# Reordering the last loads and the output projection at the end of a cached-attention decode step

## The chip, the cores and the metric

The kernel runs on one core of one Trainium2 chip. The metric is the device time of one execution in microseconds (us). The profile takes one execution; its own span is about 1.2 to 1.4 us shorter than the time of the same run. All times of events below are us from the start of that span.

Words used throughout: the attention works on half-tiles of K and V of 4 MB (4 heads of one batch row, a half of their positions). **P0** and **P1** are the last two of 32 half-tiles. In each half-tile some of the 128 key columns (positions per partition) get their scores on TensorE (transpose, copy by ScalarE, matmul with q) and the rest on VectorE (multiply, four halving adds, one reduce). A **group** is 8 key columns on TensorE. **P·V** is the matmul of the exponentials with V, the **projection** the matmul of the earlier heads' output with wo, and **gate**, **up** and **down** are the three FFN products. The earlier heads' output is the tile O_all. The **granted clock** is TensorE's clock as a share of its full speed: 1.00 is called full clock here, 0.50 half clock.

## The reference

```
h  = x + attention(layernorm(x)) @ wo      # 2 batch rows, 1 query each, 32 heads x 128,
                                           # 8192 cached keys and values per head, bf16
h2 = h + (relu(n @ W_gate) * (n @ W_up)) @ W_down    # n = layernorm(h), 512 -> 1376 -> 512
```

K and V are 268 MB of the 281 MB that have to be read, and every byte is used once.

## The kernel before

A loop works off 15 pairs of half-tiles; the last pair is written out behind it (the "tail"). The parts that matter, cut (`...`):

```python
# SP queue: loads of the last pair (o is the last pair; X is freed by VectorE of the loop)
load(K, A_k_cache, o, k_sem[0], 0, J)                   # first half of K: P0
sp.wait((d2s, 2 * o))
nc.sync.dma_start(X[:], A_wo[0:128 * DR]...)            # wo, 3.5 MB
load(K, A_k_cache, o, k_sem[1], J, 2 * J)               # second half of K: P1
sp.wait(tokp("pv", p))
load(V, A_v_cache, o, v_sem, 0, J)                      # V of P0
for k, (j0, j1) in enumerate(((V_LAST, J), (0, V_LAST))):   # V_LAST = 32
    load(V, A_v_cache, o, sem_vl[k], J + j0, J + j1)
...                                                     # then W_up, W_gate, W_down
```

```python
# TensorE, tail
k_part(tail, P0, range(2, 7), ((k2p, 1),))              # 5 groups (40 columns)
k_part(tail, P1, range(8, 13), ((k2p, 2),))
nc.tensor.wait_ge(a2p, 14); nc.tensor.wait_ge(sem_wo, 16)
for r in range(DR): ... matmul(Op[1][...], lhsT=O_all[:, r, :], rhs=X[...])   # projection, 28
pv(tail, P0, ...)
nc.tensor.wait_ge(a2p, 16)
for c in range(DC): ... matmul(Wp[...], lhsT=os_sb[strided], rhs=sel2)       # its sum, fp32
pv(tail, P1, ...)
```

```python
# ScalarE, tail: in this order
# P0: copies of 5 groups, exponentials of TensorE's columns
# P1: copies of 5 groups, exponentials of TensorE's columns, copy of O_all,
#     exponentials of P0's VectorE columns, copy of the projection, exponentials of P1's
```

The softmax here doesn't subtract the row's maximum and nothing guards it: scores larger than these inputs give would overflow.

## Time and profile before

| | before |
|---|---|
| time, median of 3 runs | 657.40 us (657.39 to 657.51) |
| span of the profile | 656.1 us |
| DMA rate, 40 to 560 us | 434 GB/s, DMA share 1.00 |
| P1's last score on TensorE | 631.7 |
| last exponential | 639.4 |
| last matmul of P·V ends | 644.4 |
| gate matmuls start | 650.36, on a DMA |

The first lines to read are the DMA rate and the DMA share: the loop is a stream of bytes that never pauses. What the engines do can only matter behind the last bytes of K, and there the reader compares two clocks: when the weights land, and when the engines are ready for them. How the time from 639 to 656 is spent shows in the view by stretches (columns: stretch, its length, busy time of PE, PEld, DVE, ACT and POOL with instruction counts, granted TensorE clock, DMA share, GB/s):

```profile
639.00:644.00 5.00, 4.51 (x50) 2.98 (x46) 0.35 (x2) 0.42 (x4) 0.00 (x0) 1.00 0.98 408
650.00:656.00 6.00, 3.60 (x93) 2.53 (x90) 1.25 (x6) 0.54 (x2) 0.00 (x0) 0.50 0.39 144
```

While P·V runs, TensorE is busy 4.51 of 5 us at the full clock, and the DMA queue is still full; it drains only in the last 6 us. So at the end of this kernel the bytes and the engines are almost level.

### The profile page before, as it was taken

To read this page: it belongs to the slowest core of one execution; us is meant where nothing else is said; L and a number is where in the kernel's file an instruction comes from. 1 tells how busy PE (TensorE), PEld (TensorE's weight loads), DVE (VectorE), ACT (ScalarE), POOL (GpSimd) and SP (SyncE) were. 2 spreads that over 40 slices of the span, in tenths; PEclk is the share of its full clock that TensorE was granted. 3 is DMA by queue.
4 is the path that set the end of the run, shared out by engine and by line. 5 is a ranking of instruction groups with operands and counts; after the bars stand their busy time and mean duration, and the time that the engine had idled before them with its cause. 6 is when DMAs were issued, how large, how long until landed. Compare 5 with 4: busy or idle time off the path is not lost.

```text
span 656.1 us, 8543 instructions
## 1 busy us (share of the span) xinstructions
PE 371.9 (57%) x3480; PEld 236.3 (36%) x3481; DVE 432.7 (66%) x275; ACT 304.6 (46%) x719; POOL 88.7 (14%) x96
## 2 busy tenths in 40 slices
PE   2374573756457385545637555474755537464677
PEld 0152441615134161423416242251623325152445
DVE  1187493947849395793939669393875939488771
ACT  1355362735536173443716445371653527254460
POOL 4000020030301103030120303003030300303000
PEclk9856556566655756665575667557565655766657
DMA  9999999999999999999999999999999999999997
GB/s 408 401 439 440 447 435 404 443 443 443 416 428 439 447 439 400 443 443 447 420 420 439 447 435 404 447 439 447 428 412 443 443 435 420 431 439 415 430 423 313
DMA packets 6324, 281.16 MB, mean 429 GB/s; under 512 B 710, under 2 KB 812, under 8 KB 1324
## 3 DMA queue, kind: packets, MB, share of 16 engines
q1 hardware_dynamic: 6308, 281.05, 99.3%
q8 instruction: 5, 0.08, 0.1%
q14 instruction: 3, 0.02, 0.0%
q10 hardware_dynamic: 8, 0.00, 0.0%
HBM read 281.05 MB, written 0.00 MB: 428 GB/s over the span
## 4 chain that ended last, share of the span: by engine, by line
DMA 64%; PE 22%; ACT 7%; DVE 6%; issue 1%; DVEq 0%; SPq 0%
DMA K<-in_A_k_cache_dram 59%; PE T L395 16%; ACT kT L578 7%; DMA K<-in_B_W_gate_dram 5%; PE S L378 5%; DVE prod L552 2%; DVE prod L561 2%; DVE X L561 1%; DVE X L552 1%; DVE scores L566 0%; PE O L816 0%; PE O L764 0%; DVEq L617 0%; DVEq L598 0%; DVE kT L824 0%
## 5 line engine op out<-in xcount | busy, mean ns | idle before, releaser
L578 ACT ACTIVATE kT<-T 128x1024 bf16<-128x1024 bf16 x160 | 160.0, 1022 | 196.5 <-PE T L395 192.7
L395 PE MATMUL T<-ident_f,K 128*128 128x128 f32 x640 | 161.7, 416 | 100.7 <-DVEq L598 94.8
L552 DVE TENSOR_TENSOR X<-K,q_c 128x11264 bf16<-128x11264 bf16 x15 | 90.4, 6026 | 172.5 <-DMA K<-in_A_k_cache_dram 172.5
L418 PE MATMUL O<-V,e 128*16 128x512 bf16 x1024 | 117.2, 596 | 111.1 <-ACT e L506 77.0
L395 PEld LDWEIGHTS T<-ident_f,K 128*128 128x128 f32 x640 | 114.5, 213 | 102.8 <-DVEq L598 96.8
L561 DVE TENSOR_TENSOR prod<-prod 128x5632 bf16<-128x5632 bf16 (+1 forms) x68 | 104.3, 1533 | 4.0
L552 DVE TENSOR_TENSOR prod<-K,q_c 128x11264 bf16<-128x11264 bf16 x17 | 102.3, 6020 | 6.2 <-DMA K<-in_A_k_cache_dram 4.5
L506 ACT ACTIVATE e<-scores 32x88 bf16<-32x88 f32 x128 | 51.1, 399 | 105.4 <-DVEq L609 103.9
L418 PEld LDWEIGHTS O<-V,e 128*16 128x16 bf16 x1024 | 30.3, 116 | 184.9 <-ACT e L506 101.8
L561 DVE TENSOR_TENSOR X<-X 128x5632 bf16<-128x5632 bf16 (+3 forms) x60 | 92.0, 1533 | 3.7
L378 PE MATMUL S<-q_c,kT 128*128 128x8 bf16 x1280 | 60.8, 171 | 40.1 <-ACT kT L578 40.0
L378 PEld LDWEIGHTS S<-q_c,kT 128*128 128x128 bf16 x1280 | 51.5, 107 | 75.6 <-ACT kT L578 73.7
L533 POOL MEMSET O_l<- 128x32 bf16 x13 | 1.7, 130 | 427.6 <-DVEq L615 427.6
L538 POOL COPY rsel<-rows 128x112 bf16<-128x112 bf16 x14 | 40.4, 2885 | 39.5 <-DVEq L615 38.7
L431 PE MATMUL Ob<-sel,os_sb 128*128 128x4 f32 x136 | 29.3, 339 | 11.0 <-ACT os_sb L581 11.0
L506 ACT ACTIVATE e<-S 32x40 bf16<-32x40 f32 x128 | 31.9, 249 | 2.4 <-PE S L378 0.9
L431 PEld LDWEIGHTS Ob<-sel,os_sb 128*128 128x128 f32 x136 | 27.8, 303 | 12.9 <-ACT os_sb L581 12.8
L506 ACT ACTIVATION_READ_ACCUMULATOR e<-scores 32x1 f32 x128 | 28.1, 219 | 0.0
L506 ACT ACTIVATION_READ_ACCUMULATOR e<-S 32x1 f32 x128 | 25.6, 200 | 1.5
L540 POOL TENSOR_TENSOR O_l<-O_cur,mask 128x32 bf16<-128x32 bf16 x14 | 23.1, 1652 | 0.0
L549 POOL COPY q_c<-q_all 128x144 bf16<-128x144 bf16 x16 | 15.2, 950 | 45.5 <-PE O L418 33.1
L578 ACT ACT_TABLE_LOAD x15 | 19.2, 1283 | 0.3
(106 smaller groups left out, 136.2 us busy)
## 6 DMA issues: line engine op xcount, KB each, us to landing
K<-in_A_k_cache_dram SPq DMA_DIRECT2D x2, 4096.0 KB, 21.8
V<-in_A_wq_dram SPq DMA_DIRECT2D x1, 4096.0 KB, 12.5
V<-in_A_v_cache_dram SPq DMA_DIRECT2D x1, 4096.0 KB, 24.9
X<-in_A_wo_dram SPq DMA_DIRECT2D x1, 3584.0 KB, 18.0
V<-in_A_v_cache_dram SPq DMA_DIRECT2D x1, 3072.0 KB, 32.1
K<-in_B_W_up_dram SPq DMA_DIRECT2D x1, 1376.0 KB, 30.1
K<-in_B_W_gate_dram SPq DMA_DIRECT2D x1, 1376.0 KB, 33.1
V<-in_A_v_cache_dram SPq DMA_DIRECT2D x1, 1024.0 KB, 33.9
```

What stands on the lines that cost most here:

```text
L378: i = nc.tensor.matmul(Sp[p % 2][:, A * jj:A * jj + 2 * A], lhsT=kv_[:, k, r, :], rhs=q_c[:, 2 * A * r:2 * A * r + 2 * A], start=(r == 0), ...
L395: i = nc.tensor.transpose(Tp[g % 2][:, k * 128:(k + 1) * 128], k_t[:, j:j + 2, :].rearrange("p j d -> p (j d)").bitcast(F32), ident_f[:])
L418: i = nc.tensor.matmul(Op[0][c:c + 16, :], lhsT=e_t[q][:, j // VJ, :], rhs=v_t[:, j:j + VJ, :].rearrange("p j d -> p (j d)"), start=(q == ...
L431: i = nc.tensor.matmul(Ob[:, 0:A], lhsT=os_sb[:, jj * Dh:(jj + 1) * Dh], rhs=sel[:, A * jj:A * jj + A], start=(jj == 0), stop=(jj == VJ - 1))
L506: i = nc.scalar.activation(out=e_t[q][h, j0 // VJ:j1 // VJ, :].rearrange("p g (j a) -> p g j a", a=A)[:, :, :, a], in_=src(h, a), func=ACT ...
L533: pool.run(e.memset(o_window(o - 1)[0], 0.0))
L538: e.tensor_copy(out=rsel[:, :, o % B, :], in_=bass.AP(x.tensor, x.offset, [list(x.ap[0]), [DR - OS, A], [1, DR]]))
L540: e.tensor_tensor(out=w, in0=O_cur[:].unsqueeze(2).broadcast_to([128, A, NM]), in1=mask[:, off // 4:off // 4 + OS // 4 * (A - 1) + 1:OS // ...
L549: nc.gpsimd.tensor_copy(out=q_c[:], in_=q_all[:, o]).then_inc(g2d, 1)
L552: return nc.vector.tensor_tensor(out=pr[:, 0:JC, :], in0=tile(K, p)[:, 0:JC, :], in1=q_c[:, Q2:QW].unsqueeze(1).broadcast_to([128, JC, Dh] ...
L561: run(nc.vector.tensor_tensor(out=pr[:, 0:JC, 0:w], in0=pr[:, 0:JC, 0:w], in1=pr[:, 0:JC, w:2 * w], op=ALU.add))
L578: to_pe(nc.scalar.activation(out=kT[gg % 2][:], in_=Tp[gg % 2][:].bitcast(BF16), func=ACT.Copy))
```

## The change

Its intent: keep the last K in one piece ahead of wo, so that the key work of both last half-tiles can run without a second wait for K; put the projection of the earlier heads between the two key parts; and take 16 of VectorE's columns of P1 over to TensorE (7 groups, 56 columns) so that VectorE ends earlier. The last V keeps its pieces of 32, 24 and 8 KB a row, with the small piece now at the other end of the columns. At the very end each engine that copies the output waits for its own slice of the last matmul group. The core of the diff (cut):

```diff
-                k_part(tail, P0, range(2, 7), ((k2p, 1),))
-                k_part(tail, P1, range(8, 13), ((k2p, 2),))
-                nc.tensor.wait_ge(a2p, 14)
+                k_part(tail, P0, range(3, 8), ((k2p, 1),))
                 nc.tensor.wait_ge(sem_wo, 16)
                 for r in range(DR): ...            # projection, unchanged
-                pv(tail, P0, ((JC, J, ((v_sem, 16),)), (0, JC, ((a2p, 15),))))
-                ...                                # sum of the projection stood here
+                def op_sum(): ...                  # the sum, called behind P1's second group
+                k_part(tail, P1, range(10, 10 + NGL), (), op_sum)      # NGL = 7
+                E1 = 10 + NGL
+                pv(tail, P0, ((JC, J, ((v_sem, 16),)), (0, JC, ((a2p, E1 + 1),))))
...
-                            load(K, A_k_cache, o, k_sem[0], 0, J)
+                            load(K, A_k_cache, o, k_sem)
                             sp.wait((d2s, 2 * o))
                             nc.sync.dma_start(X[:], A_wo[0:128 * DR]...)
-                            load(K, A_k_cache, o, k_sem[1], J, 2 * J)
...
-                    for m in range(4):
+                    for m in (0, 2, 1, 3):
                         i = nc.tensor.matmul(Op[0][32 * m:...], ...)   # last slices of down
+                        if n == FC - 1:
+                            t_y[m] = pe.run(i)
```

ScalarE's order follows: the copy of O_all moves ahead of P0's copies, the copy of the projection ahead of P1's copies.

## The prediction

> **What bounds the kernel now.** I read the page's forty slices first, then the view by stretches, the DMA issues, the waits, and last the timeline of the tail (all times below are us from the start of the span).
>
> ```profile
> DMA  9999999999999999999999999999999999999997
> GB/s 408 401 439 440 447 435 404 443 443 443 416 428 439 447 439 400 443 443 447 420 420 439 447 435 404 447 439 447 428 412 443 443 435 420 431 439 415 430 423 313
> 40.00:560.00 520.00, 298.37 (x2686) 190.69 (x2687) 360.79 (x206) 254.08 (x604) 70.39 (x62) 0.57 1.00 434
> ```
>
> The third line is the view by stretches for 40 to 560: after the times of PE, PEld, DVE, ACT and POOL come the granted clock, the DMA share and the rate. The DMA share is 1.00 at 434 GB/s for 520 us, and the slices show it full until the last one. The body of the loop is therefore a stream of bytes; nothing the engines do there shows in the time, and the change adds or removes no byte. Only the last stretch, from the arrival of the last K to the end, can move. Its arrivals, from the DMA issues (size, us from issue to landing):
>
> ```profile
> X<-in_A_wo_dram SPq DMA_DIRECT2D x1, 3584.0 KB, 18.0
> V<-in_A_v_cache_dram SPq DMA_DIRECT2D x1, 1024.0 KB, 33.9
> K<-in_B_W_up_dram SPq DMA_DIRECT2D x1, 1376.0 KB, 30.1
> K<-in_B_W_gate_dram SPq DMA_DIRECT2D x1, 1376.0 KB, 33.1
> ```
>
> With the issue times of the timeline these become landings: wo issued at 596.40, so 614.4; the last 8 KB rows of V at about 643.7; W_up issued at 616.87, so 647.0; W_gate issued at 617.24, so 650.3. The two halves of the last K land at 605.9 (VectorE starts on the first at 606.01) and 624.1. The timeline of TensorE and VectorE then shows who waits:
>
> ```profile
> 624.20 1.97 PE L395 MATMUL T<-ident_f,K 128*128 128x128 f32 x8 [5.93 <-DVEq L648]
> 624.23 6.03 DVE L552 TENSOR_TENSOR prod<-K,q_c 128x11264 bf16<-128x11264 bf16 x1 [4.50 <-DMA K<-in_A_k_cache_dram]
> 631.32 0.38 PE L378 MATMUL S<-q_c,kT 128*128 128x8 bf16 x8 [0.92 <-ACT kT L578]
> 633.94 3.16 PE L475 MATMUL O<-X,O_all 128*2 128x512 bf16 x28 [2.24 <-ACT O_all L678]
> 639.57 2.03 PE L482 MATMUL W<-sel,os_sb 128*128 128x2 f32 x8
> 641.53 1.47 PE L418 MATMUL O<-V,e 128*16 128x512 bf16 x24
> 643.82 0.61 PE L418 MATMUL O<-V,e 128*16 128x512 bf16 x8 [0.49 <-DMA V<-in_A_v_cache_dram]
> 647.98 1.72 PE L764 MATMUL S<-d_b,K 128*128 128x2 bf16 x44 [0.26 <-DVE d_b L744]
> 650.36 1.71 PE L764 MATMUL O<-d_b,K 128*128 128x2 bf16 x44 [0.18 <-DMA K<-in_B_W_gate_dram]
> 652.43 1.59 PE L816 MATMUL O<-K,hd 128*2 128x128 bf16 x40 [0.36 <-DVE hd L807]
> ```
>
> The reader is to see that the engines are nearly as late as the bytes. The last 8 matmuls of P·V wait 0.49 for V, the gate matmuls wait 0.18 for W_gate, and the W_down matmuls wait twice 0.3 for their blocks. So the compute chain behind the last K has about 0.5 us of slack at V and some 0.1 us at the gate. Whatever delays it by more than that moves the end.
>
> **What the Trainium skill says.** (1) "DMA: Bandwidth & Descriptors", section "Where 436 GB/s comes from": the port ceiling is 435 GB/s. The 434 GB/s above agrees, so larger rows cannot buy speed here. (2) The same page, "Queues, rings and completion order": each engine takes descriptors in ring order. The landings agree, they come in the order of issue, so a K issued whole ahead of wo pushes wo back by its own length. (3) "TensorE: Matmul & The Clock Gate", "What's actually happening": half clock by default, full clock after a busy window of about 3.4 us. The trace agrees: the granted clock is 0.51 in 624 to 639 and 1.00 in 639 to 644; 28 matmuls of 512 columns took 3.16 us in the first (113 ns each), 24 took 1.47 us in the second (61 ns). (4) "VectorE: DVE Perf Modes", "The perf-mode tier table": tensor_tensor in bf16 runs at two elements a cycle at most. 11264 elements in 6.03 us agree, and so a multiply of 72 columns scales nearly with its length.
>
> **The change part by part.**
>
> *Loads.* K whole: 8.4 MB, landing at 605.9 + 9.7 = 615.6 (4.2 MB at 432 GB/s is 9.7). wo then lands where the second K half landed, at 624.1. V, W_up, W_gate and W_down hold the same bytes behind the same bytes: the V pieces are 32, 24 and 8 KB rows before too, only which columns the small one carries changes. All land as before, to 0.1 us. The FFN weights are issued about 5 us later (their buffer is read until about 622 instead of 616.8), still 20 us ahead of their turn. No gap in the stream, so nothing gained there.
>
> *VectorE.* First half-tile (P0): starts at 615.65 rather than 606.01, same 13.7 us (606.01 to 619.73), ends 629.4. Second (P1) with 72 instead of 88 columns: multiply 4.95, four adds 5.2 (6.24 scaled, 0.1 fixed each), reduce 0.75: ends at 640.5, against 637.45 before. That is 3 us later, in spite of 16 columns fewer.
>
> *TensorE and ScalarE.* Before, P1's transposes began when K landed, at 624.2. Now they stand behind the wo projection in TensorE's order, and this waits for wo at 624.1. So:
> - P0's key part takes 7.5 us as at 624.20 to 631.70, from 615.65 to 623.2, then TensorE waits for wo.
> - Projection: 28 matmuls, 3.16 us, to 627.3.
> - Two groups of transposes, 1.97, to 629.3; the sum of the projection (same strided fp32 weights, 2.03), to 631.3.
> - Score of group 0 and the third group's transposes, about 1.3, so its copy begins at 632.6; from there a group costs about 1.23 (score 0.24, transposes 1.09, copy 1.02 and three handovers, two groups overlapping; 5 groups took 7.5 us). Five copies: 4 x 1.23 + 1.02 = 5.95, to 638.6; last score to 639.0. Before: 631.7. **7.3 us later.**
> - ScalarE's exponentials now all stand behind this: 56 columns from PSUM 4 x 0.49 = 1.96 (0.475 a pair with 40), P0's 88 columns 1.72 (as at 633.91 to 635.63), P1's 72 columns 1.6. They end at 641.0, 642.7 and 644.3; before, the last ended at 639.44.
> - P·V: 22 matmuls of P0 are left from 642.7, then 24 + 8 of P1 with the small zs product. 54 x 61 ns + 0.45 = 3.7 at full clock, 54 x 107 ns + 0.6 = 6.4 at half. TensorE has idled from 640 to 642.7, so it starts cold and warms within a window of 3.4 us: I take the middle, 5.1, to 647.8. Before: 644.43. **3.4 us later**, and V has long landed.
> - From the last P·V matmul to the end of the span it was 656.1 - 644.43 = 11.7. Of this about 0.1 (gate) and 0.5 (W_down) were waits for DMA that vanish, because all weights have landed by 653.7; the staged output copies (VectorE and ScalarE start after their own slice of the last matmul group instead of the last of four) save about 0.15. A cold clock in the fp32 column sum adds up to 0.8 (1.87 at half clock against 1.05), I take 0.3. So 11.2, and the end at 659.0.
>
> The span was 656.1 for a time of 657.4, 1.3 outside it. Sum: 659.0 + 1.3 = **660.3 us**, 2.9 slower, 0.4%.
>
> **The rivals.**
>
> *The bytes still set the end.* If the chain is as fast as the author hoped, W_gate at 650.3 and W_down at 653.7 end it as now, and only the staged copies show: about 657.2. For it: the stream is full to 651 and VectorE's share of P1 shrinks by 18%, with no 4.5 us wait before it. Against it: the slack is under 0.5 us, and ScalarE must run 7 copies after 627.3 and then 12 exponentials in order, which no clock of TensorE shortens by 3 us.
>
> *TensorE's clock decides.* If the 3.16 us of continuous projection warm the array and it stays warm, transposes take 0.65 (as at 614.87) instead of 1.09, groups become bound by the copy at about 1.03, the key part ends 1.4 us earlier and P·V at 61 ns: 657.6 to 658.3. If it stays cold through P·V and the column sum: 662. The trace of before shows both within each iteration of the loop.
>
> *VectorE becomes the bound.* Its P1 scores come at 640.5, before ScalarE is free for them at 642.7. It would have to be over 2 us later than worked out; then each us adds one us.
>
> *wo's wait is hidden.* If wo landed before P0's key part ends (623.2), P1 could start right behind. It lacks 0.9 us, so this rival is worth no more than that.
>
> **Range and chances.** The clock gives -2 to +2 around 660.3, the copies and exponentials perhaps half a us. Eight times in ten: 658.1 to 662.0, with more below than above left out, because the bytes put a floor near 657.2. 2% are 13 us; no part of the chain is that large: faster 0.01, same 0.98, slower 0.01.
>
> **What would show it.** In the profile after: P0's multiply at about 615.7; the projection at about 624.2 with an idle time before it put down to wo; P1's last score near 639; the last exponential near 644.3; the P·V matmuls no longer waiting for V but for ScalarE; gate and W_down matmuls without a DMA wait, the stream of DMA empty some 3 us before the last matmul. The chain that ended last should name wo's load, TensorE and ScalarE in place of W_gate's load. I am wrong if the gate matmuls still start at about 650.4 after a DMA wait, if P1's transposes start well before 627, or if the exponentials of P0 run ahead of P1's copies.

## The result

| | runs | median | range |
|---|---|---|---|
| before | 6 | 657.39 us | 657.23 to 657.58 |
| changed | 6 | 659.44 us | 658.72 to 660.42 |

The ratio is 1.0032, with a 95% interval of 1.0019 to 1.0045. (A ratio is the mean time of one kernel's runs over that of the other's of the same rounds, so not quite the ratio of the medians quoted.) All outputs are right. The changed kernel is some 2 us slower, and its runs spread over 1.7 us where the runs of before spread over 0.35: three lie from 658.72 to 658.98 and three from 659.91 to 660.42. The profiled run is one of the second three, 659.91 with a span of 658.7.

The DMA issues of the changed kernel (size, us from issue to landing):

```profile
X<-in_A_wo_dram SPq DMA_DIRECT2D x1, 3584.0 KB, 27.7
K<-in_B_W_gate_dram SPq DMA_DIRECT2D x1, 1376.0 KB, 28.1
```

wo is issued at the same moment as before (596.46 against 596.40), but takes 27.7 us instead of 18.0 and lands at 624.1: it now stands behind a second half of K. W_gate is issued 4.9 us later (622.15) and lands 5.0 us sooner after that, at 650.25, as before (650.3). The bytes are where they were. The timeline of the changed kernel's tail, TensorE, VectorE and ScalarE:

```profile
615.72 6.03 DVE L565 TENSOR_TENSOR prod<-K,q_c 128x11264 bf16<-128x11264 bf16 x1 [11.31 <-DMA K<-in_A_k_cache_dram]
624.16 3.16 PE L481 MATMUL O<-X,O_all 128*2 128x512 bf16 x28 [1.47 <-DMA X<-in_A_wo_dram]
627.25 1.97 PE L401 MATMUL T<-ident_f,K 128*128 128x128 f32 x8
629.01 1.84 PE L489 MATMUL W<-sel,os_sb 128*128 128x2 f32 x8
637.49 0.35 PE L384 MATMUL S<-q_c,kT 128*128 128x8 bf16 x8 [0.93 <-ACT kT L594]
639.73 0.75 DVE L581 TENSOR_REDUCE scores<-prod 128x72 f32<-128x576 bf16 x1
641.62 5.20 PE L426 MATMUL O<-V,e 128*16 128x512 bf16 x46 [3.04 <-ACT e L518]
647.08 0.61 PE L426 MATMUL O<-V,e 128*16 128x512 bf16 x8
653.32 1.69 PE L779 MATMUL O<-d_b,K 128*128 128x2 bf16 x44
655.36 1.24 PE L832 MATMUL O<-K,hd 128*2 128x128 bf16 x40 [0.35 <-DVE hd L822]
```

Read it beside the lines of before in the prediction. VectorE starts on P0 9.7 us later (615.72 against 606.01). The projection waits for wo, and P1's transposes stand behind it: they start at 627.25 where they started at 624.20. The last score is done at 637.84 instead of 631.7. P·V no longer waits for V but 3.04 us for ScalarE's exponentials. The gate matmuls start at 653.32 instead of 650.36 and wait for no DMA at all: W_gate has been there for 3 us. The chain of waits, which ended in W_gate's load before (33.08 us of it, from 617.24), now names wo's load and then only engines:

```profile
596.46 27.66 DMA X<-in_A_wo_dram
624.16 3.16 PE O L481 x28
627.32 1.90 PE T L401 x8
629.22 1.64 PE W L489 x8
...
641.62 5.20 PE O L426 x46
```

And the clock, from the view by stretches of the changed kernel:

```profile
639.00:644.00 5.00, 2.38 (x24) 0.84 (x28) 1.42 (x3) 3.91 (x20) 0.00 (x0) 0.58 0.99 412
650.00:656.00 6.00, 5.13 (x153) 4.76 (x154) 1.68 (x10) 0.00 (x0) 0.00 (x0) 0.50 0.37 139
```

From 639 to 644 TensorE is idle for half the time while ScalarE is busy 3.91 of 5 us, and the granted clock is 0.58 instead of 1.00. In the last stretch TensorE has 153 matmuls to do where 93 were left before: the weights are there, the engines are late.

### The profile page after: what moved, and what is told of

The parts are those of the page before. It is cut to its first block, busy times and chain, and to the rows that moved or that the text cites. A ratio compares the mean times of both kernels' runs of the same rounds, so it can differ in the third digit from the quotient of the medians.

```text
span 658.7 us, 8590 instructions
## 1 busy us (share of the span) xinstructions
PE 374.7 (57%) x3504; PEld 236.2 (36%) x3505; DVE 430.6 (65%) x275; ACT 306.4 (47%) x721; POOL 88.8 (13%) x96
## 4 chain that ended last, share of the span: by engine, by line
DMA 63%; PE 24%; ACT 8%; DVE 3%; issue 1%; SPq 0%; DVEq 0%
DMA K<-in_A_k_cache_dram 59%; PE T L401 17%; ACT kT L594 7%; PE S L384 5%; DMA X<-in_A_wo_dram 4%; DVE X L575 1%; DVE X L565 1%; DVE prod L565 1%; PE O L426 1%; ACT e L518 1%; PE O L481 0%; PE S L779 0%; PE W L489 0%; PE O L779 0%; PE O L832 0%
## 5 line engine op out<-in xcount | busy, mean ns | idle before, releaser
L594 ACT ACTIVATE kT<-T 128x1024 bf16<-128x1024 bf16 x162 | 162.1, 1023 | 194.0 <-PE T L401 190.3
L426 PE MATMUL O<-V,e 128*16 128x512 bf16 x1024 | 119.0, 603 | 115.1 <-ACT e L518 79.9
L565 DVE TENSOR_TENSOR prod<-K,q_c 128x11264 bf16<-128x11264 bf16 (+1 forms) x17 | 101.3, 5957 | 11.3 <-DMA K<-in_A_k_cache_dram 11.3
L575 DVE TENSOR_TENSOR prod<-prod 128x5632 bf16<-128x5632 bf16 (+3 forms) x68 | 103.4, 1520 | 4.0
L518 ACT ACTIVATE e<-scores 32x88 bf16<-32x88 f32 (+1 forms) x128 | 50.8, 397 | 106.1 <-DVEq L625 104.6
L439 PE MATMUL Ob<-sel,os_sb 128*128 128x4 f32 x136 | 27.7, 327 | 11.2 <-ACT os_sb L597 11.2
L518 ACT ACTIVATE e<-S 32x40 bf16<-32x40 f32 (+1 forms) x128 | 32.1, 251 | 2.4 <-PE S L384 0.9
L439 PEld LDWEIGHTS Ob<-sel,os_sb 128*128 128x128 f32 x136 | 26.2, 287 | 13.1 <-ACT os_sb L597 13.1
## 6 DMA issues: line engine op xcount, KB each, us to landing
X<-in_A_wo_dram SPq DMA_DIRECT2D x1, 3584.0 KB, 27.7
```

The lines of the kernel that those rows point to most:

```text
L426: i = nc.tensor.matmul(Op[0][c:c + 16, :], lhsT=e_t[q][:, j // VJ, :], rhs=v_t[:, j:j + VJ, :].rearrange("p j d -> p (j d)"), start=(q == ...
L439: i = nc.tensor.matmul(Ob[:, 0:A], lhsT=os_sb[:, jj * Dh:(jj + 1) * Dh], rhs=sel[:, A * jj:A * jj + A], start=(jj == 0), stop=(jj == VJ - 1))
L518: i = nc.scalar.activation(out=e_t[q][h, j0 // VJ:j1 // VJ, :].rearrange("p g (j a) -> p g j a", a=A)[:, :, :, a], in_=src(h, a), func=ACT ...
L565: return nc.vector.tensor_tensor(out=pr[:, 0:JC, :], in0=tile(K, p)[:, 0:JC, :], in1=q_c[:, Q2:QW].unsqueeze(1).broadcast_to([128, JC, Dh] ...
L575: run(nc.vector.tensor_tensor(out=pr[:, 0:JC, 0:w], in0=pr[:, 0:JC, 0:w], in1=pr[:, 0:JC, w:2 * w], op=ALU.add))
L594: to_pe(nc.scalar.activation(out=kT[gg % 2][:], in_=Tp[gg % 2][:].bitcast(BF16), func=ACT.Copy))
```

## The experiments

The theory: the bytes end as before, and the time is set by the chain wo, projection, P1's keys, exponentials, P·V, FFN, which the change made about 3 us longer. The rivals: VectorE alone is the bound; the clock is; the bytes still are. Eight kernels were run, four beside 7 runs of before (median 657.41, 657.33 to 657.62), four on another chip beside 9 runs of before (median 657.46, 657.23 to 658.05).

### The loads as before, the rest as changed

```diff
-                            load(K, A_k_cache, o, k_sem)
+                            load(K, A_k_cache, o, k_sem, 0, J)
                             ...  # wo
+                            load(K, A_k_cache, o, k2_sem, J, 2 * J)
```

TensorE and VectorE wait for `k2_sem` before P1.

> The changed kernel with the order of loads of before: first half of the last K, wo, second half of K; all else as changed (projection between the key parts, 56 columns on TensorE). Theory (the late chain of keys behind wo costs the time): wo lands at about 614.4, the projection runs from about 618 to 621.5, P1's keys start at 624.2 instead of 627.3, so the last score comes 2 to 3 us earlier (near 635) and the last exponential near 640; P.V meets V's last rows (643.7), and the time returns to 657.2 to 658.0. Rival (the projection's place or the 7 groups cost it, whatever the loads): it stays at 659 or above.

Measured: 657.71 us (657.24 to 657.95, 4 runs), ratio 1.0003 (0.9986 to 1.0020). The timeline of this kernel:

```profile
619.01 3.16 PE L482 MATMUL O<-X,O_all 128*2 128x512 bf16 x28
624.47 1.09 PE L402 MATMUL T<-ident_f,K 128*128 128x128 f32 x8 [2.30 <-DMA K<-in_A_k_cache_dram]
641.57 2.07 PE L427 MATMUL O<-V,e 128*16 128x512 bf16 x24 [0.18 <-DMA V<-in_A_v_cache_dram]
```

The projection runs while TensorE would wait for K anyway and is over 2.3 us before K comes; P·V waits for V again. The loss is gone. Projection between the key parts and 7 groups cost nothing that can be measured with these loads; they cost only where wo comes late.

### The projection behind the key parts, K whole

```diff
-                nc.tensor.wait_ge(sem_wo, 16)
-                for r in range(DR): ...                      # projection
-                k_part(tail, P1, range(10, 10 + NGL), (), op_sum)
+                k_part(tail, P1, range(9, 9 + NGL), ())
+                nc.tensor.wait_ge(sem_wo, 16)
+                for r in range(DR): ...                      # projection
                 pv(tail, P0, ...)
+                op_sum()
```

> The changed kernel with the projection put back behind P1's key part, its sum back behind P0's P.V; K still whole ahead of wo, 7 groups. Theory: P1's keys follow P0's at once (about 623.2), last score near 633, VectorE's P1 scores (640.5) become what the last exponential waits for (near 642), projection hides beside the exponentials; time 657.3 to 658.7. Rival (the late K alone costs it, through VectorE, whatever the projection's place): 659 or above.

Measured: 657.67 us (657.55 to 658.17, 4 runs), ratio 1.0006 (0.9989 to 1.0023). In its timeline the projection runs beside the exponentials, and the last exponentials wait for VectorE:

```profile
633.69 3.16 PE L489 MATMUL O<-X,O_all 128*2 128x512 bf16 x28
640.34 0.36 ACT L518 ACTIVATE e<-scores 32x72 bf16<-32x72 f32 x1 [2.17 <-DVE scores L581]
641.88 1.47 PE L426 MATMUL O<-V,e 128*16 128x512 bf16 x24 [0.86 <-ACT e L518]
```

So the place of the projection, with K whole, is worth the full loss too: two different repairs of the same chain each bring the time back. VectorE is now what the exponentials wait for, at 640.3, but that is early enough.

### K whole alone, on the kernel before

```diff
-                            load(K, A_k_cache, o, k_sem[0], 0, J)
+                            load(K, A_k_cache, o, k_sem[0])
                             ...  # wo
-                            load(K, A_k_cache, o, k_sem[1], J, 2 * J)
```

> The kernel before with one thing changed: the last K is loaded whole, ahead of wo; 5 groups, 88 columns on VectorE, projection behind the keys, as before. Theory: the late K alone costs 2 to 4 us, through VectorE: its P1 scores come at 642.7 (629.4 + 13.3), the last exponential at 644.4, 24 + 8 matmuls of P.V behind it end at 647 to 648.6 instead of 644.4; time 659.5 to 661.5. Rival (the keys wait only for TensorE's order): with the projection behind the keys nothing is lost, 657.4 to 658.

Measured: 661.40 us (660.42 to 662.00, 4 runs), ratio 1.0053 (1.0038 to 1.0069). This kernel differs from the one above in its 5 groups (88 columns on VectorE), in the place of O_all's copy on ScalarE, in the order of V's last two pieces, and in the output copies:

```profile
642.01 0.89 DVE L566 TENSOR_REDUCE scores<-prod 128x88 f32<-128x704 bf16 x1
642.93 0.40 ACT L506 ACTIVATE e<-scores 32x88 bf16<-32x88 f32 x1 [5.19 <-DVE scores L566]
644.71 2.74 PE L418 MATMUL O<-V,e 128*16 128x512 bf16 x24 [2.56 <-ACT e L506]
```

ScalarE idles 5.19 us for VectorE's scores, and P·V follows at 644.7. Loading K whole delays P0 by 9.7 us and with it VectorE, which works both half-tiles off one after the other. By itself it costs more than the whole change: 4 us. Not all of that is VectorE's lateness. P·V's 24 matmuls start 3.2 us later than before (644.71 against 641.53), and what follows runs at half clock: these 24 took 2.74 us against 1.47, the last 8 1.03 against 0.61, the fp32 column sum 1.87 against 1.05, together 2.5 us. The waits for DMA of before fall away in return. P·V ended at 648.95, later than the 647 to 648.6 expected. The kernel above, with its 56 columns on TensorE, does not have this loss; the smaller differences just named, and the other chip, are in that comparison too.

### Five groups in the changed kernel

```diff
-    NGL = 7
+    NGL = 5
```

> The changed kernel with 40 columns of the last half-tile on TensorE as before (5 groups), VectorE 88 columns. Theory: last score 2.4 us earlier (near 635.4), but VectorE's scores come at 642.7 instead of 640.5, so the last exponential is at 644.4 instead of 643.1, while only 32 matmuls of P.V are left behind it instead of 54: end about the same, 658.8 to 660.4. If TensorE and ScalarE alone set it, it would be 2.4 us faster than the change (657); if VectorE alone, 2.2 us slower (661.7).

Measured: 661.27 us (660.17 to 661.66, 4 runs), ratio 1.0053 (1.0036 to 1.0070). The expectation, 658.8 to 660.4, missed by about 1 us. Its event times were right: the last score is done at 635.31 (expected 635.4), and the last exponentials start at 643.93 and take 0.39, so they end at 644.3 (expected 644.4). What was missed is the speed behind it:

```profile
644.38 2.74 PE L426 MATMUL O<-V,e 128*16 128x512 bf16 x24 [2.66 <-ACT e L518]
647.59 1.03 PE L426 MATMUL O<-V,e 128*16 128x512 bf16 x8
649.32 1.87 PE L439 MATMUL Ob<-sel,os_sb 128*128 128x4 f32 x8 [0.70 <-ACT os_sb L597]
```

The 32 matmuls of P·V take 114 to 129 ns each and the fp32 column sum 1.87 us, all at the half clock, where the changed kernel had 0.61 us for its last 8 and 1.06 for the column sum, both at the full clock. In the changed kernel 46 matmuls stand in one row ahead of these; here 22 and 24 with a pause between. That the pause is why the full clock didn't come is likely and not tested. The time lies nearer to the 661.7 expected if VectorE alone set it. The trace speaks against that: the last exponentials end only 1.2 us later than in the changed kernel (644.3 against 643.09) and P·V 0.9 us later (648.62 against 647.69), and 0.8 us more is the column sum's slower clock. So the taking over of 16 columns by TensorE is the good part of the change, worth 1.8 us in the place where it stands, the clock included.

### The sum of the projection behind the keys

```diff
-                k_part(tail, P1, range(10, 10 + NGL), (), op_sum)
+                k_part(tail, P1, range(10, 10 + NGL), ())
+                op_sum()
```

> The changed kernel with only the sum of the projection (8 fp32 matmuls, 1.64 us on the chain of the changed kernel's profile) moved from between the second and third group of transposes to behind the last score, where TensorE idles 3.0 us for the exponentials. Theory: the last score and P0's exponentials come 1.6 us earlier, the P1 exponentials about 1.1 (VectorE's scores at 640.5), the time falls by 1.1 to 1.7 to about 657.8 to 658.4. Rival (bytes or the clock set the end): within 0.4 us of the change.

Measured: 657.65 us (657.49 to 658.17, 4 runs), ratio 1.0005 (0.9988 to 1.0021), 1.8 us below the changed kernel and a little more than expected.

```profile
627.87 6.92 ACT L595 ACTIVATE kT<-T 128x1024 bf16<-128x1024 bf16 x7
635.06 2.01 PE L489 MATMUL W<-sel,os_sb 128*128 128x2 f32 x8
640.57 0.37 ACT L519 ACTIVATE e<-scores 32x72 bf16<-32x72 f32 x1 [1.63 <-DVE scores L582]
```

In this execution ScalarE makes its 7 copies without a gap: the transposes run at the full clock (0.63 to 0.64 us for 4, against 1.09 at half) and TensorE is always ahead. The last score is done at 635.21, 2.6 us earlier than in the changed kernel's profile: 1.64 was the sum on the chain, and the rest goes with the clock. Behind it P·V ran mostly at half clock here too (0.50 from 639 to 644), and the loss is gone all the same: the earlier start was enough. The sum ran in TensorE's idle time instead, and from there VectorE limits. That leaves the sum's place as the cheapest repair: one line, and the loss is gone.

### Filler matmuls in the idle time before P·V

```diff
+                for r in range(24):      # results are not used
+                    nc.tensor.matmul(Tp[0][32 * (r % 4):32 * (r % 4) + B, :], lhsT=O_all[:, r, :],
+                                     rhs=X[:, r * D:(r + 1) * D], start=True, stop=True)
                 pv(tail, P0, ...)
```

> The changed kernel with 24 matmuls of 512 columns of no use (into a bank that is free by then) behind the last score, where TensorE idles 3.0 us before P.V. Theory that the clock is a part of it: P.V's 46 matmuls, 5.20 us at half clock in the changed kernel's profile, take 2.9 to 3.5, and the time falls by 1.2 to 2.2, to 657.3 to 658.3, and the spread of the runs shrinks. Rival (the clock is granted by chance or is no part): within 0.4 us of the changed kernel run beside it.

The changed kernel itself was run beside it:

> The changed kernel once more, for the spread of its runs and a second trace: 658.7 to 660.4 in two clusters as at first. If the clock makes the clusters, the second trace has the same last score within 1.2 us, and P.V plus column sum differ by the clock granted in them.

Measured: 658.18 us with the filler (657.35 to 658.48, 4 runs; ratio to before 1.0007), 659.67 without (659.05 to 660.37, 4 runs; 1.0029). First P·V with the filler, then P·V of the changed kernel run beside it (the first row has 10 matmuls more, which the changed kernel had run ahead of its pause):

```profile
640.14 4.54 PE L426 MATMUL O<-V,e 128*16 128x512 bf16 x56
644.93 0.61 PE L426 MATMUL O<-V,e 128*16 128x512 bf16 x8
```

```profile
642.15 5.14 PE L426 MATMUL O<-V,e 128*16 128x512 bf16 x46 [3.03 <-ACT e L518]
647.54 0.61 PE L426 MATMUL O<-V,e 128*16 128x512 bf16 x8
```

With TensorE kept busy through the wait, P·V ends at 645.54 instead of 648.15. Of these 2.6 us, 0.7 come from the earlier last score of that execution (637.70 against 638.37). The rest is P·V itself. So the clock is a real part of the loss, about 1.5 us in the time. The spread did not shrink much (1.1 us against 1.3), so that part of the expectation fell.

The second trace of the changed kernel tells where runs may differ: its last score came at 638.37, 0.5 us after that of the first trace, because in the first the full clock was granted during the first transposes behind the sum (0.64 us for 4) and in the second not (1.09). What was expected of P·V and the column sum did not come: they took the same in both (5.20 and 5.14, 1.06 and 1.06). Its 10 runs do not fall into two clusters any more, but lie from 658.7 to 660.4. That the clock makes this whole spread is likely and not shown: only two of the executions have traces, and their times are 0.5 us apart.

### The staged output copies alone, on the kernel before

The diff is the last part of the change (slices in the order 0, 2, 1, 3, each copy waiting for its slice), with 5 rounds.

> The kernel before with the staged output copies alone (VectorE and ScalarE each start when their own slice of the last matmul group is done, slices in the order 0, 2, 1, 3). Theory: 0.05 to 0.15 us faster, 657.25 to 657.4, hardly to be told from the spread of 0.3.

Measured: 657.34 us (657.30 to 657.67, 5 runs) against 657.46, ratio 0.9998 (0.9985 to 1.0012): not to be told from nothing. The trace fits this:

```profile
653.84 0.29 PE L817 MATMUL O<-wd_last,hd 96*2 96x128 bf16 x4
654.15 0.59 DVE L825 CAST kT<-O 2x128 bf16<-2x128 f32 x2 [1.82 <-PE O L817]
654.19 0.56 ACT L829 ACTIVATE kT<-O 2x128 bf16<-2x128 f32 x2 [9.15 <-PE O L817]
```

All four matmuls together take 0.29 us, and one alone takes 0.27 (266 ns is the mean of these four in the profile of before). By the profile, which models the ends of matmuls, they overlap almost wholly, so the first slice is hardly ready before the last, and VectorE starts 0.02 us behind the whole group, where before it was 0.04.

No run points to a version that beats the kernel before by more than the spread. The three repairs end at 657.65 to 657.71, and the first two of them wait for DMA again (W_down in both, twice 0.3 to 0.4 us, and V in the first), so they meet the bytes. With the sum moved, TensorE waits for no DMA in the last 18 us; there the engines still end it.

## Why the prediction was right

It gave 660.3 us, 658.1 to 662.0, and "within 2%" with 0.98; the median was 659.44. The mechanism held step by step. Its working is in the text above; here only what each step became:

| step | predicted | first profile of the changed kernel |
|---|---|---|
| VectorE starts on P0 | 615.65 | 615.72 |
| projection starts, on wo's landing | 624.1 | 624.16 |
| projection ends | 627.3 | 627.32 |
| sum ends | 631.3 | 630.85 |
| P1's last score | 639.0 | 637.84 |
| VectorE's P1 scores | 640.5 | 640.48 |
| last exponential | 644.3 | 643.09 |
| P·V ends | 647.8 | 647.69 |
| from there to the end of the span | 11.2 | 11.0 |
| end of the span | 659.0 | 658.7 |

- **Loads: right.** wo landed where the second half of K had landed, everything behind it as before.
- **VectorE: right** to 0.1 us, by scaling with the columns. It was not the bound in the changed kernel; where the other chain was shortened (projection behind, sum moved) it became what ScalarE waits for, as the rival said, without costing time there.
- **TensorE's key part: mis-sized by 1.2 us.** The prediction took the half clock for all groups. In the first profile the transposes of two groups ran in 0.64 us, and the sum took 1.64 on the chain instead of 2.0. In the second trace, with less of the full clock, the last score came at 638.37, closer to what was predicted.
- **P·V: mis-sized by 1.0 us the other way.** The prediction took the middle between full and half clock, 5.1 us. From the end of P0's exponentials (641.58) it took 6.1: the 46 matmuls ran at half clock almost throughout (113 ns each), only the last 8 at full. The two errors cancelled, so the end agrees better than the working deserves.
- **Staged copies: wrong.** The step "save about 0.15" failed; they save nothing that can be measured, by the profile the four matmuls of a group end together.
- **Rival "the bytes still set the end": refuted** by the gate matmuls, which found W_gate 3 us old, and by the stream, which drains at the same time as before.
- **Rival "the clock decides": right in kind.** It moves P·V by about 2 us, and filler matmuls recovered 1.5 us of the time.
- **Rival "wo's wait is hidden": it was not.** TensorE waited 1.47 us for wo in the first profile.

Where the loss comes from is shown by the parts, though they do not simply add. K whole costs 4 us alone, slower clock included. The 16 columns more on TensorE are worth 3.7 us where the projection stands behind the keys (657.67 against 661.40, on two chips and with the smaller differences named) and only 1.8 where it stands between them (659.44 against 661.27). A part of the difference is that the late keys there give back half of what VectorE gains: its scores come 2.2 us earlier, the last exponential 1.2. How much of the rest is the clock is open. The 2 us that are left go when the projection, or only its sum, is taken off the way to P1's keys, or when wo is loaded ahead of the second half of K again.

## What to carry to other kernels

What cost time here was the order of the loads behind which the last long engine chain starts: a transfer that moves back by one buffer takes with it everything that an engine does in order behind it, so put in-order work that waits for a late transfer behind the work that doesn't. Look for the engine's idle time (here the 3 us for the exponentials) and put side work there rather than at the head of the chain. The pause on TensorE cost twice here, once as a pause and once in the slower clock of what followed (the filler matmuls took back 1.5 us). The changed kernel's runs spread over 1.7 us, so a single run of such a tail says little about 1 us.

## What the Trainium skill lacked or had wrong

- "TensorE: Matmul & The Clock Gate", "What's actually happening": the section says that a busy window of about 3.4 us brings the full clock, and doesn't say how busy. Here the busy time did not order the clock: from 624 to 639 TensorE was busy 10.6 of the 15 us in the kernel with K whole alone, 12.1 with the sum moved and 13.9 in the second trace of the changed kernel, and the granted clock was 0.50, 0.84 and 0.57. Many of these matmuls are transposes; what the page says of transposes in another part was not weighed here.
- The same page, "LDWEIGHTS (loading the stationary operand)": the formula there has the number of columns alone. Two groups of 8 fp32 weight loads of 128 columns each, made at the full clock in the kernel before, took 1.94 us where the weights are read with a step of 4 elements (the projection's sum) and 0.97 us where they are contiguous (the column sum). At half clock the difference is small: 1.97 us with the step (the second trace of the changed kernel) against 1.78 contiguous (five groups). So the strided loads gain nothing from the full clock, and that section does not say so; the skill's notes on strided reads elsewhere were not weighed here.
- "DMA: Bandwidth & Descriptors", "Where 436 GB/s comes from": the page says there, without a condition, that for transfers between HBM and SBUF the HBM side, about 358 GB/s, binds. Here one core, with the kernel on no other, read HBM at 434 GB/s for 520 us, the fabric figure of the same section. Its 425 GB/s for a large transfer, given there too, agrees better, and a note in the section before limits the 358 to two cores that stream at once; the sentence lacks that condition.
